# Two-stage packed attention with a gated feed-forward: leftover rows of four batches together, and half of batch 1's hidden columns, through seven products in place of whole products

## The chip, the cores and the metric

One Trainium2 chip, one of its cores. The metric is the device time of one execution in microseconds (us), the median of the runs shown; smaller is better. TensorE is PE here, and PEld its weight loads; VectorE is DVE, ScalarE is ACT, GpSimd is POOL, and SyncE is SP, whose queue issues nearly all DMAs. Each engine takes its own instructions in the order in which they stand.

## The reference, cut to what matters

```python
# 8 batches, 8 heads, 576 tokens, head_dim 64, 32 packed rows; d_model 512, d_ff 2048
def sm_attn(qq, kk, vv):
    s = scale * np.matmul(qq, kk.transpose(0, 1, 3, 2))
    a = np.exp(s - np.max(s, axis=-1, keepdims=True))
    a = a / (np.sum(a, axis=-1, keepdims=True) + 1e-09)
    return np.matmul(a, vv)
p_packed = sm_attn(p, k, v)
x = sm_attn(q, p_packed, p_packed)      # then (batch * tokens, 512)
h = x @ w_in                            # (4608, 2048)
out = (h * (1.0 / (1.0 + np.exp(-h)))) @ w_out
```

All of it is float32. The kernel writes a product of two float32 matrices as three products of a rounded upper part and the remainder (hi with hi, hi with lo, lo with hi).

## The kernel before

**Tiling.** Each batch's 576 tokens are two halves of 288. A half has 256 main rows (two blocks of 128) and 32 leftover rows. The 2048 hidden columns are 16 blocks f of 128 columns, or 8 pairs p of two blocks, or 4 quarters j of four blocks. PE makes a block of h for one half with six products of 288 columns (`h_products`, L615). ACT applies the gate. The leftover rows go to the tile `rest`, which has room for two batches (`b % 2`).

**Whole products.** For batches 0 and 1, each (batch, block) is a unit: `out_products` multiplies 128 x 128 blocks of the gated h by 512 columns of w_out, three terms for each of four row blocks, so 12 matmuls of 512 columns (L673). There are 32 such units. The sums of the first half of the columns are written to DRAM (`parts`) and added later.

**Seven products.** For batches 2 to 7, a unit is (batch, half, pair). The 2 x 2 blocks (two row blocks by two hidden blocks) times the 2 x 2 blocks of w_out (two hidden blocks by two column halves of 256) take seven block products, three terms each: 21 matmuls of 256 columns (`pair_products`, L673). What goes into them is combined first: on the side of h by three POOL instructions (`pair_sums`, L647 to L649), on the side of w_out once per pair on DVE, POOL and ACT (`pair_of_w`, `sums_of_pair`, `sums_upper`, `sums_lower`). The latter are kept in DRAM (`keep_sums`) and read back for each unit (`load_sums`, 768 KB) into a ring of four tiles; one of them replaces half of a block of w_out in SBUF (`first_in_place`). ACT rounds the seven combined blocks (`all_upper`, L663) and DVE makes the remainders (`all_lower`, L667). Four PSUM banks (`acc`) collect a half of a batch; then `pair_rows` (one ACT copy, L816, and five DVE additions, L815) makes the rows and stores them.

**Leftover rows.** After each odd batch, and once for batches 0 and 1, the 128 leftover rows of two batches go through `rest_products`: 16 blocks with three terms of 512 columns, 48 matmuls, in units of four blocks. `rest_rows` adds two banks where needed and stores four strips of 32 rows.

**Order.** `ORDER` is a string of some 1,700 steps that are recorded one by one, so that it sets the order on PE, DVE, ACT and SP by hand; POOL's order follows from it too. A step's letter names the function and its number the unit: B and G, N, I, F, L, O are `h_products`, the gate, leftover rows, `pair_sums`, `all_upper`, `all_lower` and `pair_products` (or the leftover products); E is `pair_rows`, Y `rest_rows`, S `load_sums`; r, R, ru, rl, rk and T are the steps of the sums of w_out.

Of the kernel before, what the change touches and what calls it, by code (L numbers as in the profile page):

```python
# [9 lines left out]
F32 = mybir.dt.float32  # L10
F32R = mybir.dt.float32r
# [8 lines left out]
P = 128  # L20
# [22 lines left out]
PACKS += [(b, j * FJ, FJ) for b in range(EARLY, B) for j in range(NJ)]  # L43
FROM_RING = [NJ] * EARLY + [2] + [0] * (B - EARLY - 1)
# [93 lines left out]
def packed_attention_ffn(ctx: ExitStack, tc: tile.TileContext, pkT, qT, v, w_in, w_out, out):  # L138
# [100 lines left out]
    class Weights:  # L239
# [8 lines left out]
        def fetch(self, n):  # L248
# [5 lines left out]
            elif place == "last":  # L254
                raw = self.tiles[n - 1][:, 2 * DM :]
            else:
                raw = win[:, place : place + 2 * nf].rearrange("p f i n -> p (f i n)")
# [689 lines left out]
```

## Time and profile before

| | |
|---|---|
| median of 3 runs | 680.04 us (679.95 to 680.74) |
| profiled execution | 681.22 us, of which the span is 679.4 us |
| busy | PE 97%, PEld 86%, DVE 63%, ACT 62%, POOL 34% of the span |
| DMA | 178.62 MB, mean 263 GB/s |

The page's busy share of PE is modelled and counts overlapping records, so the table alone doesn't say how close PE is to its limit; the distance between the starts of its matmuls does, and the chain of what released what shows where PE was itself the last to be waited for. The profiled execution is 1.18 us above the median. All sums are differences that are taken against its 679.4 us of span, and carried to the median.

### The profile page before, as it was taken

The numbers are of one execution on the slowest core, as the hardware profiler recorded it, in microseconds if no ns is written. First come the engines' busy times: TensorE is split into PE (matmuls) and PEld (weight loads), VectorE is DVE, ScalarE is ACT, GpSimd is POOL, SyncE is SP. The second block draws the span as 40 slices with busy tenths as digits, with TensorE's granted clock in tenths as the row PEclk, the third lists the DMA queues.
The fourth block names the chain that finished last, engine by engine and source line by source line (L and its number), as shares of the span: only waits on it lengthen the run. The fifth ranks groups of instructions, "written<-read, shape, count | busy, mean of one in ns | idle before, by whom it ended". The sixth has DMA issues, their size and how long they took to land.

```text
span 679.4 us, 14828 instructions
## 1 busy us (share of the span) xinstructions
PE 660.8 (97%) x5980; PEld 584.2 (86%) x5980; DVE 428.9 (63%) x595; ACT 423.3 (62%) x706; POOL 229.1 (34%) x337
## 2 busy tenths in 40 slices
PE   8898999999999999999999999999999999999997
PEld 6676778787878998899888998899988999899995
DVE  4999999987784356653576428763567426663433
ACT  4798876757557456764466638684367644766442
POOL 1111213243222543444242533445341343444440
PEclk9999999999999999999999999999999999999999
DMA  9748284968688669877798477977889278767441
GB/s 360 321 158 332 71 325 121 335 232 328 241 317 311 226 264 371 330 291 268 269 354 312 132 293 274 368 272 270 325 299 363 81 263 302 247 251 259 166 171 46
DMA packets 55107, 178.62 MB, mean 263 GB/s; under 512 B 21760, under 2 KB 25856, under 8 KB 47360
## 3 DMA queue, kind: packets, MB, share of 16 engines
q1 hardware_dynamic: 54944, 177.56, 70.9%
q8 instruction: 47, 0.77, 0.4%
q10 hardware_dynamic: 96, 0.13, 0.1%
q14 instruction: 20, 0.16, 0.1%
HBM read 149.42 MB, written 24.12 MB: 255 GB/s over the span
## 4 chain that ended last, share of the span: by engine, by line
PE 72%; DVE 9%; ACT 8%; DMA 4%; issue 4%; SPq 2%; POOL 1%; ACTq 0%; DVEq 0%; POOLq 0%
PE ps_acc L673 42%; PE ps_two L615 23%; PE ps_two L304 6%; DMA win<-in_w_out 2%; DVE g_lo L633 2%; SPq L388 2%; DMA sums_of_w<-sums_of_w 1%; ACT g_hi L663 1%; DVE g_lo L667 1%; DVE o L815 1%; PE ps_two L408 1%; ACT g L626 1%; DMA w_raw<-in_w_out 1%; ACT L188 1%; ACT g_hi L627 1%
## 5 line engine op out<-in xcount | busy, mean ns | idle before, releaser
L667 DVE TENSOR_TENSOR g_lo<-g,g_hi 128x896 fp32r<-128x896 f32 x96 | 108.5, 1134 | 132.5 <-ACT g_hi L663 129.7
L673 PE MATMUL ps_acc<-wo_hi,g_hi 128*128 128x256 f32 (+1 forms) x576 | 183.0, 318 | 0.7 <-DVE o L815 0.7
L673 PE MATMUL ps_acc<-wo_hi,g_lo 128*128 128x256 f32 (+1 forms) x576 | 182.1, 316 | 0.7 <-DVE g_lo L633 0.6
L673 PE MATMUL ps_acc<-wo_lo,g_hi 128*128 128x256 f32 (+1 forms) x576 | 181.4, 315 | 0.0
L615 PE MATMUL ps_two<-a_hi,pw_hi 128*128 128x288 f32 x512 | 152.0, 297 | 0.8 <-ACT tm L331 0.3
L615 PE MATMUL ps_two<-a_hi,pw_lo 128*128 128x288 f32 x512 | 150.9, 295 | 0.0
L615 PE MATMUL ps_two<-a_lo,pw_hi 128*128 128x288 f32 x512 | 150.6, 294 | 0.2 <-DVE a_lo L546 0.2
L647 POOL TENSOR_TENSOR g<-g 128x128 f32<-128x128 f32 x96 | 51.8, 540 | 273.1 <-ACT g L637 241.1
L663 ACT CAST g_hi<-g 128x896 fp32r<-128x896 f32 x96 | 90.0, 941 | 77.0 <-POOL g L649 40.6
L673 PEld LDWEIGHTS ps_acc<-wo_hi,g_hi 128*128 128x128 f32 x576 | 108.2, 188 | 14.8 <-issue 6.9
L673 PEld LDWEIGHTS ps_acc<-wo_hi,g_lo 128*128 128x128 f32 x576 | 108.3, 188 | 10.2 <-DVE g_lo L633 2.4
L673 PE MATMUL ps_acc<-sums_of_w,g_hi 128*128 128x256 f32 x576 | 115.6, 282 | 1.0 <-DMA sums_of_w<-sums_of_w 1.0
L673 PEld LDWEIGHTS ps_acc<-wo_lo,g_hi 128*128 128x128 f32 x576 | 108.2, 188 | 6.6 <-DVE wo_lo L297 0.3
L615 PEld LDWEIGHTS ps_two<-a_hi,pw_hi 128*128 128x128 f32 x512 | 96.3, 188 | 7.1 <-issue 3.0
L673 PEld LDWEIGHTS ps_acc<-sums_of_w,g_hi 128*128 128x128 f32 x576 | 87.8, 188 | 15.0 <-issue 13.3
L615 PEld LDWEIGHTS ps_two<-a_lo,pw_hi 128*128 128x128 f32 x512 | 96.4, 188 | 1.4 <-DVE a_lo L546 0.4
L615 PEld LDWEIGHTS ps_two<-a_hi,pw_lo 128*128 128x128 f32 x512 | 96.2, 188 | 0.0
L637 ACT ACTIVATE g<-ps_two 128x512 f32<-128x512 f32 x96 | 57.1, 598 | 42.9 <-PE ps_two L615 22.7
L673 PE MATMUL ps_acc<-sums_of_w,g_lo 128*128 128x256 f32 x288 | 80.0, 278 | 0.0
L648 POOL TENSOR_TENSOR g<-g 128x256 f32<-128x256 f32 x96 | 73.1, 763 | 6.5
L649 POOL TENSOR_TENSOR g<-g 128x128 f32<-128x128 f32 x96 | 56.7, 592 | 6.5
L673 PEld LDWEIGHTS ps_acc<-sums_of_w,g_lo 128*128 128x128 f32 x288 | 54.2, 188 | 0.4 <-DVE g_lo L667 0.4
(131 smaller groups left out, 838.1 us busy)
## 6 DMA issues: line engine op xcount, KB each, us to landing
sums_of_w<-sums_of_w SPq DMA_DIRECT2D x96, 768.0 KB, 6.4
w_quarter<-w_in SPq DMA_DIRECT2D x22, 1024.0 KB, 7.2
kvq_t<-in_v SPq DMA_DIRECT2D x8, 1280.0 KB, 9.3
kvq_t<-in_pkT SPq DMA_DIRECT2D x7, 1216.0 KB, 10.4
out<-o SPq DMA_DIRECT2D x16, 512.0 KB, 3.6
kvq_t<-in_qT SPq DMA_DIRECT2D x7, 1152.0 KB, 8.4
w_raw<-in_w_in SPq DMA_DIRECT2D x6, 1024.0 KB, 8.1
sums_of_w<-w_sums SPq DMA_DIRECT2D x8, 768.0 KB, 4.6
```

The lines of the kernel that those rows point to most:

```text
L188: nc.scalar.activation(ready, ident[:, :1], (AF.Exp, AF.Silu)[n])
L304: nc.tensor.matmul(bank(par)[NP * i : NP * i + NP], lhs(r, i), rhs(r, i), start=True, stop=True)
L388: nc.sync.dma_start(self.e1T[NP * at : NP * at + NP, : some.shape[1], i], some)
L615: nc.tensor.matmul(bank, p[:, par, cols], a[:, par], start=(n == 0), stop=(n == len(todo) - 1))
L633: nc.vector.tensor_tensor(g_lo[:, c], g[:, c], g_hi[:, c].bitcast(F32), ALU.subtract)
L637: nc.scalar.activation(g[:, : 4 * P].rearrange("p (e s) -> p e s", e=2), made["h", u, None][..., :MAIN], AF.Silu)
L647: nc.gpsimd.tensor_tensor(x[:, 4], x[:, 0], x[:, 2], ALU.subtract)
L648: nc.gpsimd.tensor_tensor(x[:, 5:7], x[:, 0:5:4], one, ALU.subtract)
L649: nc.gpsimd.tensor_tensor(x[:, 7], x[:, 3], x[:, 6], ALU.add)
L663: nc.scalar.copy(both[0], g)
L667: nc.vector.tensor_tensor(g_lo, g, g_hi.bitcast(F32), ALU.subtract)
L673: nc.tensor.matmul(out, g[:, rows], w, start=(first and n == 0), stop=(last and n == 2), skip_group_check=True)
```

## The change

Nothing in the arithmetic of the reference is left out. What changes:

- `WHOLE = 6`: 24 units of whole products stay (batch 0, and the first half of batch 1's columns). The second half of batch 1's columns becomes 8 units of seven products (2 halves x pairs 4 to 7), whose rows are added to what `parts` holds (`main_rows`).
- The leftover rows of four batches form 256 rows, so that they can go through seven products: 8 units for batches 0 to 3 and 8 for batches 4 to 7, in place of four groups of 48 matmuls. `keep_rest` writes the leftover rows of the first two batches of each four to DRAM, `load_rest` reads them back, `copy_rest` (two ACT copies per unit) puts both pairs of batches side by side. For the last eight of these units DVE does `pair_sums`, not POOL.
- The sums of w_out lie in four places of w_in's own buffer, which is free after the packs of batch 1; the last four pairs of a group that the next group begins with aren't read again (`PAIRS` turns the order), so 76 loads in place of 96.
- Batch 2 reads all of its w_in from DRAM (24 fetches in place of 22).
- `ORDER` is another string throughout. In the last unit the four banks end in another order (`final`), and the last store has eight strips, four of them issued by ACT.

```diff
+WHOLE = 6
+PAIRS = (0, 1, 2, 3, 4, 5, 6, 7), (4, 5, 6, 7, 0, 1, 2, 3)
+FROM_RING = [NJ] * EARLY + [0] * (B - EARLY)
...
-    units = [(b, f) for b, g in BLOCKS for f in range(g * FJ, g * FJ + FJ)]
+    units = [(b, f) for b, g in BLOCKS[:WHOLE] for f in range(g * FJ, g * FJ + FJ)]
     n_early = len(units)
-    units += [(0, f, "rest") for f in range(0, NF, FJ)]
+    units += [(1, (hf, p)) for hf in range(2) for p in range(NPAIR // 2, NPAIR)]
     for b in range(EARLY, B):
-        units += [(b, (hf, p)) for hf in range(2) for p in range(NPAIR)]
-        if b % 2:
-            units += [(b - 1, f, "rest") for f in range(0, NF, FJ)]
+        units += [(b, (hf, p)) for hf in range(2) for p in PAIRS[(b + hf + 1) % 2]]
+        if b % 4 == 3:
+            units += [(b - 3, ("rest", p)) for p in PAIRS[0]]
...
+    def copy_rest(u):
+        b, (_, p) = units[u]
+        g = hidden[u] = in_turn(gp_main, [P, 8 * P], F32, "g")
+        g = g[:, : 4 * P].rearrange("p (e r s) -> p r e s", e=2, r=2)
+        nc.scalar.copy(g[:, 0], made["rest", b // 4][:, 2 * p : 2 * p + 2])
+        nc.scalar.copy(g[:, 1], rest[:, 2 * p : 2 * p + 2].rearrange("p f e h s -> p f (e h s)"))
...
-        x = summed_tiles[b, hf, p] = in_turn(tp, [P, 2, 3 * HALF], F32R, "sums_of_w", TP_BUFS)
-        nc.sync.dma_start(x.bitcast(F32), sums_of_w[p])
+        if "sums" not in made:
+            made["sums"] = win_pool.tile([P, TP_BUFS * n], F32R, name="w_sum", tag=f"win_{NF - FJ}")
+        x = made["sums"][:, p % TP_BUFS * n : p % TP_BUFS * n + n]
+        summed_tiles[p] = x.rearrange("p (t n) -> p t n", t=2)
+        nc.sync.dma_start(summed_tiles[p].bitcast(F32), sums_of_w[p])
...
+    def rest_rows(n):
+        o = pair_rows(n, "rest", n == 1)
+        for k in range(2):
+            for m in range(4):
+                at = (4 * n + 2 * k) * S + m * HS + MAIN
+                (nc.scalar if n and m % 2 else nc.sync).dma_start(out[at : at + REST], o[m * REST : m * REST + REST, k])
```

Where this moves instructions is seen at three places. First PE at the program's end, where the last half of batch 7 gives way to leftover rows (`ps_acc_2221` to `2224` before and `1971` to `1974` after are the banks 0 to 3). Before:

```order
L673 MATMUL ps_acc_2224<-sums_of_w,g_hi 128x256 x2
L673 MATMUL ps_acc_2224<-sums_of_w,g_lo 128x256
L673 MATMUL ps_acc_2224<-wo_hi,g_hi 128x256
L673 MATMUL ps_acc_2224<-wo_lo,g_hi 128x256
L673 MATMUL ps_acc_2224<-wo_hi,g_lo 128x256
L673 MATMUL ps_acc_2221<-wo_hi,g_hi 128x512
L673 MATMUL ps_acc_2221<-wo_lo,g_hi 128x512
L673 MATMUL ps_acc_2221<-wo_hi,g_lo 128x512
L673 MATMUL ps_acc_2223<-wo_hi,g_hi 128x512
```

After, the last rows of PE's program:

```order
L689 MATMUL ps_acc_1971<-wo_hi,g_lo 128x256
L689 MATMUL ps_acc_1971<-w_sum,g_hi 128x256 x2
L689 MATMUL ps_acc_1971<-w_sum,g_lo 128x256
L689 MATMUL ps_acc_1974<-w_sum,g_hi 128x256 x2
L689 MATMUL ps_acc_1974<-w_sum,g_lo 128x256
L689 MATMUL ps_acc_1974<-wo_hi,g_hi 128x256
L689 MATMUL ps_acc_1974<-wo_lo,g_hi 128x256
L689 MATMUL ps_acc_1974<-wo_hi,g_lo 128x256
L689 MATMUL ps_acc_1973<-wo_hi,g_hi 128x256
L689 MATMUL ps_acc_1973<-wo_lo,g_hi 128x256
L689 MATMUL ps_acc_1973<-wo_hi,g_lo 128x256
```

Before, 48 matmuls of 512 columns into banks 0 and 2 stand at the end; after, eight times 21 matmuls of 256 columns into all four banks, the last three of them into bank 2.

Second, DVE at the same place. `g_lo` is the remainder that the next product needs, L815 the additions of `pair_rows`. Before, to the end of the program:

```order
L667 TENSOR_TENSOR g_lo<-rest,g_hi 128x512
L815 TENSOR_TENSOR o<-ps_acc_2222,o 128x2x256
L815 TENSOR_TENSOR o<-ps_acc_2221,o 128x256
L815 TENSOR_TENSOR o<-ps_acc_2224,o 128x256
L815 TENSOR_TENSOR o<-ps_acc_2223,o 128x256
L815 TENSOR_TENSOR o<-ps_acc_2224,o 128x512
L667 TENSOR_TENSOR g_lo<-rest,g_hi 128x512 x3
L800 TENSOR_TENSOR o<-o 128x256
L801 TENSOR_TENSOR o<-ps_acc_2223,o 128x512
```

After, from the additions that end batch 7 on (L653 to L655 are `pair_sums`):

```order
L815 TENSOR_TENSOR o<-ps_acc_1972,o 128x2x256
L815 TENSOR_TENSOR o<-ps_acc_1971,o 128x256
L815 TENSOR_TENSOR o<-ps_acc_1974,o 128x256
L815 TENSOR_TENSOR o<-ps_acc_1973,o 128x256
L815 TENSOR_TENSOR o<-ps_acc_1974,o 128x512
L653 TENSOR_TENSOR g<-g 128x128
L654 TENSOR_TENSOR g<-g 128x256
L655 TENSOR_TENSOR g<-g 128x128
L683 TENSOR_TENSOR g_lo<-g,g_hi 128x896 x2
```

Before, one remainder stands ahead of the five additions and three behind; after, the sums of a unit stand between the additions and the next remainder, and such sums go on to the end, which is five more additions in place of two.

Third, DVE where the last sums of w_out are made (`w_pair` and `w_sums` are the first and the last DVE step of a pair). Before:

```order
L768 TENSOR_TENSOR w_sums<-w_pair,w_sums 128x1024
L751 TENSOR_TENSOR w_pair<-wo_hi,wo_lo 128x2x256
L751 TENSOR_TENSOR w_pair<-wo_hi,wo_lo 128x512
L633 TENSOR_TENSOR g_lo<-g,g_hi 128x512
L530 TENSOR_TENSOR tm<-tm,sm 128x576
L534 STREAM_TRANSPOSE tm<-tm 128x576
L633 TENSOR_TENSOR g_lo<-g,g_hi 128x512
L768 TENSOR_TENSOR w_sums<-w_pair,w_sums 128x1024
L786 TENSOR_TENSOR o<-ps_acc,o 128x1024 x2
L667 TENSOR_TENSOR g_lo<-rest,g_hi 128x512
```

After, at the sixth pair's last step:

```order
L783 TENSOR_TENSOR w_sums<-w_pair,w_sums 128x1024
L766 TENSOR_TENSOR w_pair<-wo_hi,wo_lo 128x2x256
L766 TENSOR_TENSOR w_pair<-wo_hi,wo_lo 128x512
L587 TENSOR_TENSOR pw_lo<-ps_two,pw_hi 128x2x512
L683 TENSOR_TENSOR g_lo<-g,g_hi 128x896
L800 TENSOR_TENSOR o<-ps_acc,o 128x1024 x2
L527 TENSOR_REDUCE sm<-tm 128x18
L528 TENSOR_SCALAR sm<-sm 128x18
L529 RECIPROCAL sm<-sm 128x18
L783 TENSOR_TENSOR w_sums<-w_pair,w_sums 128x1024
L683 TENSOR_TENSOR g_lo<-g,g_hi 128x896
```

Before, all eight pairs' sums stand ahead of the first seven-product unit, and four units of leftover rows lie between; after, pairs 4 to 7 are made first, the last of them stands between the remainders of the first and the second such unit, and pairs 2 and 3 follow later.

## Rows read from the trace of the kernel before

**Rows 1.** The page's busy times (share, instructions) and its slices of granted clock.

```profile
PE 660.8 (97%) x5980; PEld 584.2 (86%) x5980; DVE 428.9 (63%) x595; ACT 423.3 (62%) x706; POOL 229.1 (34%) x337
...
PEclk9999999999999999999999999999999999999999
```

**Rows 2.** Chain in order of time: start us, us, what and how many.

```profile
134.32 2.95 PE ps_acc L673 x12
...
187.70 8.19 PE ps_acc L673 x36
...
217.78 2.39 PE ps_acc L673 x21
...
435.50 2.68 PE ps_acc L673 x21
...
441.34 4.78 PE ps_acc L673 x42
446.12 1.58 PE ps_two L615 x12
...
518.98 10.90 PE ps_acc L673 x48
```

**Rows 3.** PE by shape: busy us, mean ns | idle before us, what ended it.

```profile
L673 PE MATMUL ps_acc<-sums_of_w,g_hi 128*128 128x256 f32 x576 | 115.6, 282 | 1.0 <-DMA sums_of_w<-sums_of_w 1.0
...
L673 PE MATMUL ps_acc<-wo_hi,g_hi 128*128 128x512 f32 x192 | 76.8, 400 | 0.7 <-DVE o L815 0.7
```

**Rows 4.** Windows: us, then busy (count) of PE, PEld, DVE, ACT, POOL, PEclk, DMA share, GB/s.

```profile
0.00:20.00 20.00, 16.70 (x222) 13.88 (x223) 10.48 (x24) 10.15 (x19) 2.06 (x8) 1.00 0.92 367
...
20.00:140.00 120.00, 112.05 (x944) 88.06 (x943) 113.81 (x161) 94.65 (x162) 29.61 (x24) 1.00 0.65 236
0.00:217.78 217.78, 206.53 (x1689) 164.52 (x1690) 181.21 (x257) 156.32 (x263) 52.57 (x55) 1.00 0.72 268
```

**Rows 5.** DVE by shape, columns as in rows 3.

```profile
L667 DVE TENSOR_TENSOR g_lo<-g,g_hi 128x896 fp32r<-128x896 f32 x96 | 108.5, 1134 | 132.5 <-ACT g_hi L663 129.7 <-PE ps_two L615 2.5
...
L633 DVE TENSOR_TENSOR g_lo<-g,g_hi 128x512 fp32r<-128x512 f32 x28 | 25.5, 912 | 9.8 <-ACT g_hi L627 9.8
...
L815 DVE TENSOR_TENSOR o<-ps_acc,o 128x512 f32<-128x512 f32 x24 | 16.4, 684 | 7.1 <-ACT o L816 7.1
L815 DVE TENSOR_TENSOR o<-ps_acc,o 128x256 f32<-128x256 f32 x36 | 14.1, 421 | 1.7
...
L667 DVE TENSOR_TENSOR g_lo<-rest,g_hi 128x512 fp32r<-128x512 f32 x16 | 10.9, 683 | 10.3 <-ACT g_hi L663 10.3
...
L418 DVE TENSOR_TENSOR pp<-ps_two,rd 128x128 f32<-128x128 f32 x7 | 2.0, 285 | 5.5 <-PE ps_two L408 5.5
...
L800 DVE TENSOR_TENSOR o<-o 128x256 f32<-128x256 f32 x4 | 1.6, 412 | 3.5 <-ACT o L799 3.5
```

**Rows 6.** Chain of the last 20 us, columns as in rows 2.

```profile
662.46 0.38 ACT o L816
...
664.23 11.21 PE ps_acc L673 x48
...
675.46 0.70 DVE o L801
...
676.18 0.40 ACTq L808
...
676.63 0.43 ACTq L808
```

**Rows 7.** DMA issues: count, KB each, median us to landing.

```profile
sums_of_w<-sums_of_w SPq DMA_DIRECT2D x96, 768.0 KB, 6.4
...
sums_of_w<-w_sums SPq DMA_DIRECT2D x8, 768.0 KB, 4.6
...
out<-o ACTq DMA_DIRECT2D x2, 64.0 KB, 2.0
```

More of the change, by code (lines that the diff above doesn't have):

```diff
@@ L572, in upper @@
             if self.f % FJ == 0:
-                pool = pw_b if b >= EARLY and j >= 2 else pw
+                pool = pw_b if b >= EARLY and j < 2 else pw
                 both = [in_turn(pool, [P, 2 * JW + 2 * AT_PW], F32R, name) for name in ("pw_hi", "pw_lo")]
@@ L658, in all_upper @@
         g = all_of(u)
-        at = 0 if g.shape[1] > FJ * P else 64 - AT_G
         both = [in_turn(gp_main, [P, 7 * P], F32R, name) for name in ("g_hi", "g_lo")]
-        both = [t[:, at : at + g.shape[1]] for t in both]
         hidden[u] = g, *both
@@ L703, in packed_attention_ffn @@
     low, high = slice(0, HALF), slice(HALF, DM)
-    def rest_products(u):
-        b, f, _ = units[u]
-        first, last = f == 0, f + FJ == NF
-        for n in sorted(range(FJ), key=lambda n: n % 2) if last else range(FJ):
-            bank = 0 if n % 2 == 0 and (f + n) // 2 in summed else 2
-            begun = opened.get(("rest", b, bank))
-            opened["rest", b, bank] = True
-            products(acc[bank], u, f + n, n, not begun, last and n >= FJ - 2)
     opened = {}
@@ L718, in pair_products @@
         g_hi, g_lo = hidden[u][-2:]
-        last = p == NPAIR - 1
+        last = is_last(u)
+        final = last and u == len(units) - 1
         def term(bank, cols, at, w_hi, w_lo):
-            key = "pair", b, hf, bank
+            key = b, hf, bank
             begun = opened.get(key)
@@ L734, in pair_products @@
         term(0, high, 4, *t(2))
-        term(2, low, 6, *w(f2, high))
+        if not final:
+            term(2, low, 6, *w(f2, high))
         term(3, low, 1, *t(1))
         term(3, high, 3, *w(f1, high))
+        if final:
+            term(2, low, 6, *w(f2, high))
     summed_tiles = {}
@@ L794, in store, with pair_rows @@
         nc.sync.dma_start(out[at : at + MAIN].rearrange("(k p) e -> p k e", p=P), o)
-    def rest_rows(b):
-        o = in_turn(osb, [P, 2, DM], F32, "o")
-        if opened.get(("rest", b, 0)):
-            nc.scalar.copy(o[:, 1], acc[0])
-            nc.vector.tensor_tensor(o[:, 1, high], o[:, 1, high], o[:, 1, low], ALU.add)
-            nc.vector.tensor_tensor(o[:, 0], acc[2], o[:, 1], ALU.add)
-        else:
-            nc.scalar.copy(o[:, 0, low], acc[2][:, low])
-            nc.vector.tensor_copy(o[:, 0, high], acc[2][:, high])
-        for n in range(4):
-            at = b * S + n * HS + MAIN
-            rows = slice(n * REST, n * REST + REST)
-            (nc.scalar if n % 2 and b == B - 2 else nc.sync).dma_start(out[at : at + REST], o[rows, 0])
-    def pair_rows(b, hf):
+    def pair_rows(b, hf, final=False):
         o = in_turn(osb, [P, 2, DM], F32, "o")
```

226 lines of the change are left out of this document (123 added, 103 removed).

## The prediction

> **What bounds the kernel now.** I read the page's busy times first: PE is busy 97% of the span at full granted clock throughout (2.4 GHz), no other engine above 63% [rows 1]. A modelled busy share is not yet a bound, so I read the chain in order of time next, for the distance at which matmuls follow each other: 42 of 256 columns in 4.78 us, so 0.1138 us each; 48 of 512 columns in 10.90 us and 36 in 8.19 us, so 0.227 us each; 12 of 288 columns in 1.58 us [rows 2]. A whole product thus costs exactly two halves, and the time goes by columns. PE by shape shows how little PE stands still between these: a wait of 1.0 us in all ahead of the products with loaded sums, of 0.7 us ahead of the leftover products [rows 3]. So from about 40 us on the kernel is a string of matmuls with few gaps, and columns that are taken away come off the end, if the others keep up.
>
> Whether they can is asked where they are nearest to PE. That is DVE early on: it is busy 113.81 of the 120 us from 20 to 140, 95%, while it prepares the weights [rows 4]. Later it has much room (428.9 us in all).
>
> **The change part by part.** The sums are differences against the profiled execution's 681.22 us (span 679.4), which stands 1.18 us over the median; I carry them to the median of 680.04.
>
> *PE's columns.* Removed: 8 units of batch 1 with 12 matmuls each, and four groups of 48 for leftover rows, 288 of 512 columns: 288 x 0.227 = 65.4 us. Added: 8 + 16 units of 21, 504 of 256 columns: 504 x 0.1138 = 57.4 us. Net -8.0. The bounds are the prices of a run that begins after other work: 2.95 us for 12 instead of 2.73, 2.68 us for 21 instead of 2.39 [rows 2]. With all of batch 1's old units dear, 23.6 + 43.6 - 57.4: -9.8; with all new units dear, 65.4 - 64.3: -1.1. I take -8.0, since runs of both kinds stand between the same h products before and after.
>
> The Trainium skill has a rule against this: "TensorE: Matmul & The Clock Gate", section "Back-to-back issue gap", says that a stream of weight loads and matmuls settles at some 81 ns for 128 columns and 131 ns for 512. By it, 288 wide ones are 37.7 us and 504 halves, estimated from that page at 98 ns between those two, 49.4 us: +11.7. The trace disagrees with it (0.227 us for 512 columns), and the trace decides.
>
> *DVE early.* The first seven-product unit of batch 2 starts at 217.78 us now, and until then DVE is busy 181.2 us [rows 4]. Counted in the order, DVE has nearly the same ahead of that unit after: all weights, all eight pairs' sums and the same attention; 8 remainders of 896 columns more (9.1), 8 of 512 fewer (7.3), four of leftover rows fewer (2.7), two sets of five additions more (2 x (2 x 0.684 + 3 x 0.421) = 5.3), one set of leftover additions (1.1), a transpose and a pack remainder (2.0, an estimate from rows of like width) fewer: +1.3, so 182.5 us [rows 5]. But PE gets there sooner. Ahead of it stand 144 matmuls of 512 columns fewer (32.7), 170 of 256 more (19.3) and 12 of 288 fewer (1.6): 15.0 us, so at 202.8. By 140 us DVE has done 10.5 + 113.8 = 124.3 [rows 4]; the other 58.2 must fit into 62.8 us, 93%. The most that the trace shows over a long stretch is the 95% above; from 140 to 217.78 it was 56.9 of 77.8, 73%, when it had to wait for PE. I take 90%, since a unit's remainder waits for ACT's rounding and, here, POOL's sums: 64.7 us, +2.0. Bounds: -1 (a start that is a little earlier) to +8 (82%).
>
> In the same place stand the sums of pairs 4 to 7. The last is made just ahead of the second new product's remainder; from there it must be written (4.6 us) and read back (6.4 us) for the fourth product [rows 7], 11.0 us behind each other in SP's queue, with a read of `parts` between. PE has some 14.5 us of work from there if DVE is in time (three products at 2.39, four h products at 1.58, scores of an estimated 1.0), so it is hidden; if PE already waits for that remainder, the cover is 10.4 and a wait of 1 to 2 us shows. It is in the bounds above.
>
> *Leftover rows.* The two copies on ACT per unit (32, near 0.4 us each by the 0.38 us copy in rows 6) and the eight DMAs that keep and read rows are in stretches where ACT and DMA have room (ACT 62% busy); without that cover they would cost 12 us of ACT, in part. SP's queue gets these DMAs and two more weight fetches, and loses 20 of 96 loads of 768 KB [rows 7]. PE's 1.0 us of waiting for loads could go [rows 3]; against it two more groups now end in banks that the next product wants, and a dense run of leftover units makes each remainder follow the one before closely. I take +0.4, between -1 and +2.
>
> *DVE at the last group.* Behind the last half of batch 7 DVE has five additions (2.6 us), then one unit's sums (2 x 0.285 + 0.412 = 1.0, by the rows of like width) and a remainder (1.13), before the second leftover unit can go on [rows 5]. The copy and the first additions begin some 1.0 us before PE is through with that half, since banks 1 and 0 end nine matmuls early; so the remainder is there about 4.1 us after PE's last matmul of batch 7. PE has one unit (2.39), the wait for the first bank and two matmuls in the meantime, 2.7: a wait of 1.4. Before, the same place cost 0.7 by rows 3 and ended at 664.23 in rows 6. From there on a unit costs DVE 2.1 and PE 2.39, so it keeps up, with few tenths lost. +0.6, between 0 and +3.
>
> *The end.* Before, one addition of 0.70 us and ACT's two issues of 0.40 and 0.43 us stand behind PE's last matmul, then a landing of 2.0 [rows 6, 7]. After, five additions (2.6) and the copy (0.38) with 1.0 us of them ahead of PE's end: 2.0, so +1.3; four issues on ACT for two: +0.8. Together +2.1, between +1.3 and +2.6.
>
> Sum: -8.0 + 2.0 + 0.4 + 0.6 + 2.1 = -2.9, so 680.04 - 2.9 = **677.1** (the profiled execution 678.3).
>
> **The rivals.** *DVE keeps up.* For it: 95% over 120 us before, and 4.5 us of room in the count above. Against it: more engines stand in a row ahead of each remainder. Only columns and end count: -8.0 + 2.1 = -5.9, 674.1.
>
> *DVE is the bound until batch 2, but not by far.* At 85% the 58.2 us take 68.5 in place of 62.8, +5.7 in place of +2.0: 680.8, no change.
>
> *Slower: PE waits for DVE from 140 us to the first unit of batch 2.* For it: 73% there before. Against it: that was idle time for want of work. The point from which it decides is a busy share of 84%, where the wait (6.5 us) and the other terms eat up the columns; at 80% it is 72.8 us, +10.0: 685.1.
>
> *The products do not get cheaper.* If all 24 new units are dear (a run that is cut up by waits for remainders), columns give -1.1 only: 684.0. For it speaks that leftover units now need seven combined blocks each; against it that rows of 4.78 for 42 are the usual ones. The skill's rule named above would end on this side as well.
>
> **How the numbers follow.** Forecast, 675.4 to 678.6: 0.46. DVE keeps up, 672.6 to 675.4: 0.24. DVE the bound by a little, 678.7 to 681.3: 0.14. DVE the bound by far: 0.11. Products not cheaper: 0.05, of which 0.01 for the rule. No bound is under 672.6 but that of dear old units. The range of 8 in 10 is 672.6 to 681.5. What a measurement can tell from no change is about 0.2%, 1.4 us: faster 0.70, same 0.14, slower 0.16.
>
> **What would show it.** Right: products of 256 columns at 0.114 us, 504 more of them; DVE over 88% busy from 140 us to the first unit of batch 2, which starts near 205; a wait of PE of 1 to 2 us behind batch 7's last addition; some 6 us from PE's last matmul to the end where it is 4 now. Wrong: that unit starting behind 209 us (DVE), PE idle ahead of products with `w_sum` as the releaser (the loads), or new units at 2.6 us or more.

## The result: slower by 1.2%

| | before | after |
|---|---|---|
| median | 680.0 us (4 runs, 679.59 to 680.74) | 688.31 us (4 runs, 687.33 to 689.12) |
| ratio | | 1.012, 95% interval 1.0103 to 1.0138 |
| profiled execution, its span | 681.22 us, 679.4 us | 689.12 us, 687.3 us |

The forecast was 677.1 us, between 672.6 and 681.5. The page's busy times of the kernel after, beside [rows 1]:

```profile
PE 655.5 (95%) x6196; PEld 589.1 (86%) x6196; DVE 457.8 (67%) x631; ACT 426.0 (62%) x727; POOL 268.5 (39%) x385
```

PE is 5 us less busy and the span is 8 us longer, so PE waits. PE by shape says where, beside [rows 3] (columns as there); first the products for h in the kernel before, then the groups after:

```profile
L615 PE MATMUL ps_two<-a_hi,pw_hi 128*128 128x288 f32 x512 | 152.0, 297 | 0.8 <-ACT tm L331 0.3 <-ACT rest L628 0.3
```

```profile
L620 PE MATMUL ps_two<-a_hi,pw_hi 128*128 128x288 f32 x512 | 152.8, 299 | 7.8 <-ACT g L642 3.5 <-ACT rest L646 1.9 <-DVE tm L450 0.9
...
L689 PE MATMUL ps_acc<-w_sum,g_hi 128*128 128x256 f32 x720 | 144.5, 282 | 3.6 <-DMA w_sum<-sums_of_w 2.5 <-DVE o L815 1.2
...
L689 PE MATMUL ps_acc<-w_sum,g_lo 128*128 128x256 f32 x360 | 100.7, 280 | 2.9 <-DVE g_lo L683 2.9
```

The first products for h (L615 before, L620 after) waited for 0.8 us before; now it is 7.8 us, most of it for the gate on ACT (L642, L646). Where in time this is, the windows show (columns as in [rows 4]); first the kernel before, then after:

```profile
140.00:180.00 40.00, 40.00 (x270) 32.74 (x269) 31.59 (x41) 29.15 (x47) 11.39 (x11) 1.00 0.77 287
180.00:220.00 40.00, 40.00 (x278) 32.06 (x277) 26.67 (x36) 24.14 (x40) 10.51 (x15) 1.00 0.78 285
```

```profile
20.00:140.00 120.00, 113.00 (x949) 88.58 (x947) 115.64 (x162) 93.68 (x161) 31.88 (x24) 1.00 0.71 264
140.00:180.00 40.00, 34.26 (x246) 28.81 (x245) 30.06 (x36) 21.97 (x35) 20.86 (x24) 1.00 0.85 297
180.00:220.00 40.00, 36.55 (x333) 31.95 (x332) 34.37 (x41) 25.78 (x44) 22.54 (x30) 1.00 0.90 315
```

Up to 140 us the two kernels are alike. From 140 to 220 us PE (first pair of numbers) was never idle before, and is idle for 9.2 us of 80 after.

For the whole span I use PE's lag: the time at which a matmul starts, less the time that all matmuls ahead of it take at the spacings of [rows 2] (0.1138 us for 256 columns, and so on). It grows only where PE waits or where matmuls follow each other at more than these spacings. Its level depends on what the small products of the attention are priced at, so only its growth and the differences of the two kernels are read.

| | matmuls at full pace | lag at 160 us | at 220 | at 640 | at the last matmul | from there to the end |
|---|---|---|---|---|---|---|
| before | 640.4 | 23.6 | 24.2 | 33.4 | 34.8 | 4.4 |
| after | 632.3 | 21.9 | 34.9 | 45.4 | 48.7 | 6.45 |
| after less before | -8.1 | -1.7 | | | | +2.1 |
| growth from the column ahead | | | +12.4 | +1.3 | +1.9 | |

The terms add to +7.9 us, the difference of the spans. The columns came off as forecast, and 12.4 us were lost between 160 and 220 us: some 9 us are idle time of PE, the rest is matmuls at more than the usual spacing. Some 7 of the 12.4 us fall between 160 and 180 us.

### The profile page after: what moved, and what is told of

Same layout as the page of the kernel before. It is cut to its first block, busy times and chain, and to the rows that moved or that the text cites. A ratio compares the mean times of both kernels' runs of the same rounds, so it can differ in the third digit from the quotient of the medians.

```text
span 687.3 us, 15374 instructions
## 1 busy us (share of the span) xinstructions
PE 655.5 (95%) x6196; PEld 589.1 (86%) x6196; DVE 457.8 (67%) x631; ACT 426.0 (62%) x727; POOL 268.5 (39%) x385
## 4 chain that ended last, share of the span: by engine, by line
PE 64%; DVE 18%; DMA 6%; ACT 5%; issue 3%; POOL 3%; SPq 0%; DVEq 0%; ACTq 0%; POOLq 0%
PE ps_acc L689 37%; PE ps_two L620 22%; PE ps_two L310 4%; DMA w_sum<-sums_of_w 3%; DVE g_lo L683 2%; DVE o L815 2%; DMA first_sums<-w_sums 2%; ACT g_hi L679 1%; DVE g_lo L638 1%; DMA sums_of_w<-w_sums 1%; PE ps_two L414 1%; DVE win L291 1%; DVE w_raw L279 1%; DVE w_sums L783 1%; DVE w_raw L275 1%
## 5 line engine op out<-in xcount | busy, mean ns | idle before, releaser
L683 DVE TENSOR_TENSOR g_lo<-g,g_hi 128x896 fp32r<-128x896 f32 x120 | 137.5, 1150 | 142.2 <-ACT g_hi L679 140.0
L689 PE MATMUL ps_acc<-wo_hi,g_hi 128*128 128x256 f32 (+1 forms) x576 | 171.5, 298 | 1.2 <-DVE o L803 1.1
L689 PE MATMUL ps_acc<-wo_lo,g_hi 128*128 128x256 f32 (+1 forms) x576 | 170.4, 296 | 0.0
L679 ACT CAST g_hi<-g 128x896 fp32r<-128x896 f32 x120 | 112.3, 941 | 86.8 <-POOL g L655 54.1
L620 PE MATMUL ps_two<-a_hi,pw_hi 128*128 128x288 f32 x512 | 152.8, 299 | 7.8 <-ACT g L642 3.5
L653 POOL TENSOR_TENSOR g<-g 128x128 f32<-128x128 f32 x112 | 60.4, 539 | 247.5 <-ACT g L642 239.6
L620 PE MATMUL ps_two<-a_hi,pw_lo 128*128 128x288 f32 x512 | 151.2, 295 | 0.0
L620 PE MATMUL ps_two<-a_lo,pw_hi 128*128 128x288 f32 x512 | 150.7, 294 | 0.4 <-DVE a_lo L552 0.4
L689 PE MATMUL ps_acc<-w_sum,g_hi 128*128 128x256 f32 x720 | 144.5, 282 | 3.6 <-DMA w_sum<-sums_of_w 2.5
L689 PEld LDWEIGHTS ps_acc<-w_sum,g_hi 128*128 128x128 f32 x720 | 109.7, 188 | 20.1 <-issue 9.4
L620 PEld LDWEIGHTS ps_two<-a_hi,pw_hi 128*128 128x128 f32 x512 | 96.4, 188 | 17.8 <-PE ps_two L310 4.5
L689 PE MATMUL ps_acc<-w_sum,g_lo 128*128 128x256 f32 x360 | 100.7, 280 | 2.9 <-DVE g_lo L683 2.9
L620 PEld LDWEIGHTS ps_two<-a_lo,pw_hi 128*128 128x128 f32 x512 | 96.4, 188 | 1.3 <-DVE a_lo L552 0.6
L620 PEld LDWEIGHTS ps_two<-a_hi,pw_lo 128*128 128x128 f32 x512 | 96.3, 188 | 0.0
L642 ACT ACTIVATE g<-ps_two 128x512 f32<-128x512 f32 x104 | 61.4, 598 | 42.9 <-DVE g_lo L683 25.7
L654 POOL TENSOR_TENSOR g<-g 128x256 f32<-128x256 f32 x112 | 85.1, 762 | 7.4
L655 POOL TENSOR_TENSOR g<-g 128x128 f32<-128x128 f32 x112 | 72.4, 649 | 7.5
L689 PEld LDWEIGHTS ps_acc<-w_sum,g_lo 128*128 128x128 f32 x360 | 67.7, 188 | 4.2 <-DVE g_lo L683 3.9
```

The costliest lines, as they stand in the source:

```text
L620: nc.tensor.matmul(bank, p[:, par, cols], a[:, par], start=(n == 0), stop=(n == len(todo) - 1))
L642: nc.scalar.activation(g[:, : 4 * P].rearrange("p (e s) -> p e s", e=2), made["h", u, None][..., :MAIN], AF.Silu)
L653: engine.tensor_tensor(x[:, 4], x[:, 0], x[:, 2], ALU.subtract)
L654: engine.tensor_tensor(x[:, 5:7], x[:, 0:5:4], one, ALU.subtract)
L655: engine.tensor_tensor(x[:, 7], x[:, 3], x[:, 6], ALU.add)
L679: nc.scalar.copy(both[0], g)
```

## What PE waits for between 140 and 220 us

Pairs are numbered from 0, and the changed kernel makes their sums in the order 0, 1, 4, 5, 6, 7, 2, 3; those of 0, 1 and 4 are done by 140 us, and the five others are called late here. (The section on the change says that 4 to 7 are made first: 0 and 1 stand ahead of them.) What the expectations call the sixth and the seventh pair are pairs 6 and 7.

What PE waited for from 140 to 220 us (waited for, us in total, times, longest us), after; before, that list is empty:

```profile
PE ps_two L620 <- ACT g L642: 3.5, 1, 3.5
PE ps_two L620 <- ACT rest L646: 1.9, 2, 1.2
PE ps_acc L689 <- DVE g_lo L683: 1.5, 2, 1.3
PE ps_acc L689 <- DMA w_sum<-sums_of_w: 1.0, 1, 1.0
```

Two more waits for DVE, of 0.8 and 0.4 us, make it 9.1 us: 5.4 for ACT, 2.7 for DVE, 1.0 for a load.

The chain in order of time, after, from the write of pair 5's sums past the first product that reads pair 7's sums back (at 186.12 us; columns as in [rows 2]; L779 is ACT's rounding of a pair's sums, L783 DVE's remainder, L771 to L774 POOL's sums of w_out, L653 to L655 the sums of h, L679 the rounding of the combined blocks):

```profile
145.16 11.18 DMA first_sums<-w_sums
...
156.45 1.06 ACT w_sums L779
...
157.53 1.24 DVE w_sums L783
...
160.23 0.74 POOL w_pair L771
...
162.67 0.73 POOL w_pair L774
163.40 0.43 POOL g L653
...
165.20 0.95 ACT g_hi L679
...
167.18 2.35 DVE o L800 x2
...
170.74 1.66 DVE w_sums L783
...
172.42 7.42 DMA sums_of_w<-w_sums
...
179.85 6.23 DMA w_sum<-sums_of_w
...
195.38 1.39 DVE w_sums L783
196.78 1.54 DVE g_lo L683
198.31 1.47 DVE w_pair L766 x2
```

There is one tile `w_sums`. ACT can't round the next pair's sums until the two writes of the pair before have landed. The one of 256 KB takes 11.2 us here; in the kernel before its median was 4.7:

```profile
first_sums<-w_sums SPq DMA_DIRECT2D x8, 256.0 KB, 4.7
```

Behind that rounding in ACT's order stands the gate of the first seven-product unit, then comes POOL, which sums pair 7 of w_out ahead of that unit's blocks, and ACT waits again, with the gate of the next unit behind it. PE's h products run out of PSUM tiles. (In the written order that unit's sums, I24, stand ahead of pair 7's, R7. `ORDER` fixes PE, DVE, ACT and SP alone, so POOL took them the other way round; the section on the kernel before says that POOL's order follows from it, which does not hold here.) The waits of ACT from 140 to 220 us, after:

```profile
ACT g_hi L679 <- POOL g L655: 7.3, 3, 4.2
ACT w_sums L779 <- DMA first_sums<-w_sums: 4.5, 1, 4.5
...
ACT w_sums L779 <- POOL w_pair L774: 3.0, 1, 3.0
```

ACT's two longest groups in the same stretch before were for PE and for DVE:

```profile
ACT g L626 <- PE ps_two L615: 7.0, 4, 3.9
ACT g L626 <- DVE g_lo L633: 4.1, 3, 2.3
```

That speaks for a row of waits (theory A) and against DVE as the bound (theory B, the forecast's). It is not the whole case: DVE is 75% and 86% busy in the two windows, and the chain lies mostly on DVE from 193 to 202 us. The runs tell the two apart.

## The experiments

Each is the changed kernel with the edit that its text names; e4 and e5 take back half of the change, and e12, e16 and e18 join edits. "Over before" is the difference from the runs of the kernel before on the same chip.

| | median us | over before | ratio, 95% interval |
|---|---|---|---|
| changed kernel | 688.31 | +8.3 | 1.012 (1.0103 to 1.0138) |
| e1 POOL in written order | 687.09 | +7.3 | 1.0105 (1.008 to 1.013) |
| e2 sums in place | 687.34 | +7.6 | 1.011 (1.0095 to 1.0125) |
| e3 later loads | 687.14 | +7.4 | 1.0109 (1.0094 to 1.0124) |
| e4, e5 batch 1 whole | 697.71, 700.23 | +17.9, +19.9 | 1.0277 (1.0252 to 1.0302), 1.0298 (1.0281 to 1.0316) |
| e6 less DVE, 3 pairs | 688.46 | +8.1 | 1.0121 (1.0073 to 1.0168) |
| e7 e6 and e3 | 685.73 | +5.4 | 1.0078 (1.0061 to 1.0095) |
| e8 parts on POOL | 687.63 | +7.3 | 1.0102 (1.0086 to 1.0118) |
| e9 no late sums | 681.04 | +0.4 | 1.0008 (0.9998 to 1.0018) |
| e10 last sums on POOL | 691.36 | +10.7 | 1.0158 (1.0142 to 1.0173) |
| e11 more PE | 691.9 | +11.3 | 1.0154 (1.0129 to 1.0179) |
| e12 mends | 693.46 | +12.8 | 1.0192 (1.0177 to 1.0207) |
| e13 less DVE, 5 pairs | 687.34 | +6.5 | 1.0095 (1.0076 to 1.0114) |
| e14 no POOL sums | 687.12 | +6.3 | 1.0099 (1.0083 to 1.0115) |
| e15 no writes | 686.91 | +6.1 | 1.0094 (1.0078 to 1.0109) |
| e16 mends 2 | 685.72 | +4.9 | 1.0077 (1.0061 to 1.0094) |
| e17 e14 and e15 | 681.84 | +1.7 | 1.0029 (1.0018 to 1.004) |
| e18 ACT's order | 686.89 | +6.8 | 1.0092 (1.0079 to 1.0105) |

Most times lie inside a range that was stated for them or up to 0.5 us outside the nearer one. e7 and e13 fit none of theirs, e10 lost more than its text allowed, and e4, e5 and e12 lie far above what was hoped for.

### One wait at a time, with the whole result: e1, e2, e3, e8

> POOL takes its instructions in the order of the written steps; only this differs from the changed kernel (688.3 us). There the sums of the first seven-product unit stood on POOL behind the sums of w_out of the seventh pair, which came late. Theory A (the row of steps that makes the sums of w_out for pairs 5 to 7 is what PE waits for between 160 and 220 us: one tile that is free only when its write has landed, POOL's order, the read back): PE's first wait of 4.0 us falls to about 1, but the seventh pair's sums come some 2 us later and with them the wait for the loaded sums; 685 to 687 us. Theory B (DVE has too much work until batch 2, and every wait removed ahead of it comes back as one for DVE): within 1 us of 688.3.

```diff
-engines={E.PE, E.DVE, E.Activation, E.SP}
+engines={E.PE, E.DVE, E.Activation, E.SP, E.Pool}
```

> The sums of pairs 6 and 7 are made where they are needed: three quarters in their place of w_in's buffer, the fourth in w_out's block. They are still written to DRAM for later, but nobody waits for that write, and they are not read back for the first use. Theory A: ACT's wait of 4.5 us for the write of the pair before goes, and so does the wait of PE for the loaded sums of pair 7 (1.2 us); 682 to 685 us. Theory B: DVE has one instruction more for each of the two pairs and nothing less, so 687.5 to 689 us.

In `sums_upper`, for pairs 6 and 7:

```diff
+x = made["x", p] = made["sums"][:, p % TP_BUFS * n : p % TP_BUFS * n + n].rearrange("p (t n) -> p t n", t=2)
+nc.scalar.copy(x[:, 0], r[:, : 3 * HALF])
+nc.scalar.copy(wo_hi[:, 2 * p, high], r[:, 3 * HALF :])
...
```

> Two DMAs of 1.0 and 1.2 MB (the last quarter of w_in on its way out, and the k of batch 3) are issued behind the writes of the sums of pairs 5 and 6, where they stood ahead of them or at their side. Theory A: the write of pair 5 lands in 6 to 7 us in place of 11.2, ACT's wait for it (4.5 us) falls under 1, and the first wait of PE by up to 3; 685 to 687 us. Theory B: 688 us as before, since the work of DVE is the same.

```diff
-aM2.1 x3 B24 rk5 ru6 o22 l23 o23 Z0. aN2.1 k3 G24
+aM2.1 B24 rk5 x3 ru6 o22 l23 o23 Z0. aN2.1 G24
-pf11 rk6 I25
+pf11 rk6 k3 I25
```

> Batch 1's two additions of the stored first half of its columns (1.45 and 1.23 us on DVE at 191.8 and 209.9 us, each ahead of a remainder that PE waits for) go to POOL; only the store waits for them. Theory B: PE's waits behind them fall by 1.5 to 2.5 us, 685.8 to 687. Theory A: under 0.7 us, since POOL is behind ACT there and makes the next sums later.

```diff
-nc.vector.tensor_tensor(o, o, outs.pop(("o", b, hf)), ALU.add)
+nc.gpsimd.tensor_tensor(o, o, outs.pop(("o", b, hf)), ALU.add)
```

Each came out some 1 us under the changed kernel, with intervals that overlap its own, so none is a gain that is clear by itself. The profiles say why. In e2 and e3 PE's wait for the gate at 164 us fell from 3.5 to 2.2 and 2.1 us and the one of 1.0 us for pair 7's loaded sums went, but 0.9 us of waiting for the banks that `main_rows` frees came in its place. In e1 POOL made the first unit's blocks early, and ACT's 7.3 us of waiting for them went; but ACT then stood 8.3 us in two waits for landed writes (4.5 in the changed kernel) and 2.8 for POOL's sums of w_out (3.0), and PE's longest wait, now 4.0 us, came a few us later. In e8 PE's waits for DVE's remainders fell from 1.5 to 0.3 us, and the 3.5 us for the gate stayed. This fits neither theory well: waits move along the row.

### Half of the change alone: e4, e5

> One half of the change alone: batch 1's columns stay whole products as in the kernel before, the leftover rows of four batches go through seven products as in the changed one; the steps stand as in the kernel before until batch 2, and as in the changed one behind it (which half of the pairs comes first is exchanged). Columns: 192 of 512 less (43.6 us), 336 of 256 more (38.2), -5.4 us against the kernel before. Theory A or B: the loss between 160 and 220 us is from batch 1's half, so it is gone here; with +2.1 at the end and some 3 us of waits further on 679.5 to 682 us. Rival C (the leftover rows and what they need, the loads among it, make the loss): 685 us or more.

> As e4 (batch 1's columns as whole products, leftover rows of four batches through seven), with two things put right: the four DMAs that keep the leftover rows of batches 4 and 5 follow the exchange of the pairs' halves (in e4 some rows were stored too early), and the first packs of batch 2 are fetched and made some 20 us earlier, since in e4 PE waited 3.7 us for fetches of w_in, and the lag that e4 took between 190 and 240 us (16 us, with 0.72 of the clock at its lowest) was from there. If batch 1's half is what costs the 12 us between 160 and 220 us: 680 to 684 us, with PE's lag at 220 us within 3 of the kernel before. If leftover rows cost it: above 686.

```diff
-WHOLE = 6
+WHOLE = 8
-PAIRS = (0, 1, 2, 3, 4, 5, 6, 7), (4, 5, 6, 7, 0, 1, 2, 3)
+PAIRS = (4, 5, 6, 7, 0, 1, 2, 3), (0, 1, 2, 3, 4, 5, 6, 7)
-    units += [(1, (hf, p)) for hf in range(2) for p in range(NPAIR // 2, NPAIR)]
...
```

By their times both lie on the rival's side, far above it even. To 180 us the lag is that of the kernel before (23.3 and 23.0), so the loss at 160 to 180 us is from batch 1's half. Then both lose 16 to 19 us by 240 us. The longest of PE's waits there are for w_in, which the packs of batch 2 need, 3.7 us in e4 and 7.2 in e5; the rest is shorter waits for ACT and DVE, and the granted clock fell (0.76 and 0.83 from 200 to 220 us). PE's waits in e5 from 180 to 240 us:

```profile
PE ps_two L309 <- DMA w_quarter<-w_in: 7.2, 2, 3.9
```

The changed kernel reads all of batch 2's w_in from DRAM into one buffer, and the leftover rows of batches 0 and 1, which stood there before and probably gave time for it (no run takes that apart), have moved to batch 3. What the leftover rows' part would bring under an order of its own stays open.

### The sums of w_out: e9, e6, e13, e14, e15, e17, e7

> The sums of w_out of pairs 5, 6, 7, 2 and 3 are left out altogether (on DVE, POOL and ACT, with their writes and the reads into w_out's blocks); where they would be read, those of pair 4 are, so the number and size of the reads stay. Batches 1 to 7 are wrong by that. Theory D (it is the making of these sums, on whichever engine, beside the first seven-product units that takes the 12 us between 160 and 220; DVE's part and the writes' part are each only a piece, as e6, e3 and e7 show): PE's lag at 220 us falls from 34.9 to 24 to 27, 678 to 681 us. Rival E (the eight units would lose it even so: the row ACT, POOL, ACT, DVE for each unit is too long for PE's pace): lag above 30, 683 or more.

The two lines in the middle stand at the head of the six functions that make a pair's sums, `pair_of_w` to `first_in_place`.

```diff
+LEFT_OUT = (5, 6, 7, 2, 3)
...
+        if p in LEFT_OUT:
+            return
...
-        nc.sync.dma_start(summed_tiles[p].bitcast(F32), sums_of_w[p])
+        nc.sync.dma_start(summed_tiles[p].bitcast(F32), sums_of_w[4 if p in LEFT_OUT else p])
```

7.9 of 8.3 us are gone, and the lag at 220 us is 27.5. So the making of these five pairs' sums beside the first seven-product units is what makes the kernel slower than before. It is not the whole of the 12.4 us: e9 still loses some 3.5 us more than the kernel before between 160 and 220 us, nearly all of it behind 180 us. With the later terms that uses up the 8.1 us of columns, so even without these sums the change gains nothing. Then each of its parts alone:

> DVE's additions and remainders for the sums of w_out of pairs 7, 2 and 3 are cut to 16 of 256 columns each (the sums are wrong there, and batches 1 to 7 with them); every other engine and every DMA is left as it is in the changed kernel. DVE has 6 us less between 160 and 206 us (per pair 0.69 + 0.69 + 1.23 down to some 0.6). Theory B (DVE is the bound there): PE's lag at 220 us falls by 4 to 6 us, 682 to 684 us. Theory A (the chain of waits for DMA, POOL and ACT): less than 1.5 us, 686.5 to 688.

> e6 for all five late pairs (5, 6, 7, 2, 3): DVE's three instructions for each are cut to 16 of 256 columns, POOL, ACT and every DMA stay, in the same order; the sums are wrong by it. 2.0 us of DVE less for each pair, 10 us in all. All five left out on every engine gave 7.3 us (e9). If DVE alone made that loss: 681 to 682.5 us, PE's lag at 220 us near 27.5. If it is one of several: 684 to 686.5, lag 30 to 33.

```diff
+            n = SHORT if p in (5, 6, 7, 2, 3) else HALF
-            nc.vector.tensor_tensor(to, each(wo_hi, f), each(wo_lo, f), ALU.add)
+            nc.vector.tensor_tensor(to[..., :n], each(wo_hi, f)[..., :n], each(wo_lo, f)[..., :n], ALU.add)
...
```

> POOL's four instructions for the sums of each of the five late pairs are left out (3.0 to 3.7 us each, 16 us in all); DVE, ACT and all DMAs stay, and the sums are wrong. If POOL's share in the row is what holds the first units' combined blocks and with them ACT and PE: 682 to 685 us, and the first wait of 3.7 us at 164 us gone. If POOL only passes on what DVE and the writes make late: 686.5 or more.

> The writes of the sums of the five late pairs and the reads into w_out's blocks are left out, with SP's waits for them; the loads read the sums of pair 4 in their place (wrong sums). DVE, POOL and ACT do all they did. If waiting for landed writes is the larger part: 682 to 685 us, lag at 220 us under 31. If it is as small as in e2 and e3, where only its longest waits were taken: 686 to 687, lag 32 to 33.

Both leave out a function's body for the five pairs, as in e9: `sums_of_pair` in e14, `keep_sums` and `first_in_place` in e15, where the loads read pair 4's sums instead. (In e6, e7, e13 to e15 and e17 `w_pair` and `w_sums` are also allocated once, not anew for each pair.) Each of e13, e14 and e15 is within 2.2 us of the changed kernel, with intervals that overlap its own; e6 gave nothing that can be told from it. The waits of ACT from 140 to 220 us say what is next late, in e14:

```profile
ACT w_sums L785 <- DMA first_sums<-w_sums: 7.7, 3, 3.7
```

and in e15:

```profile
ACT g_hi L680 <- POOL g L656: 7.1, 3, 4.0
```

Without POOL's sums ACT stands longer for the writes (4.5 us in the changed kernel); without the writes it stands for POOL as long as there (7.3), and 4.5 us in place of 3.0 for POOL's sums of w_out. So both had to go:

> e14 and e15 together: for the five late pairs POOL's sums and the writes (with the reads into w_out's blocks) are left out; DVE and ACT do all their work for them, 10 us of DVE and 5 of ACT. Alone they gave 1.1 and 1.4 us, the same cut on DVE 1.0, all together (e9) 7.3. If what PE waits for is ACT, which stands in its order for POOL's sums and for landed writes with the gate of the next block behind it: 680.5 to 682.5 us, lag at 220 us under 29, although DVE has its full work. If DVE's work is a limit of its own behind these two: 684 us or more, lag above 31.

It gave 6.6 of the 8.3 us, with all of DVE's work in place. DVE in the stretch from 140 us to the first unit of batch 2 (columns as in [rows 4]), changed kernel, then e13, then e17:

```profile
140.00:210.35 70.35, 63.15 (x519) 53.51 (x517) 57.59 (x70) 41.74 (x69) 39.23 (x48) 1.00 0.86 298
```

```profile
140.00:209.53 69.53, 64.21 (x521) 55.32 (x519) 47.21 (x70) 42.53 (x72) 35.94 (x48) 0.98 0.88 314
```

```profile
140.00:202.28 62.28, 62.18 (x521) 53.59 (x519) 55.69 (x70) 42.10 (x71) 27.41 (x32) 1.00 0.70 256
```

Each ends where that unit starts: 210.4, 209.5 and 202.3 us. In e13 DVE has 10 us less to do and is busy 68%, and PE is hardly sooner (at a clock of 0.98). In e17 DVE has its full work, is busy 55.69 of 62.28 us, 89%, and PE is idle for 0.1 us. Theory B falls as the main cause. The loss at 160 to 180 us goes with POOL's sums and the writes, and the step between them and PE is ACT, which stood for both; e17 takes the two out together with the read-back of the late sums, so it doesn't price them one by one. The longest wait of PE that is left in e17 is for DVE, just behind that stretch, and as long as in the changed kernel:

```profile
PE ps_acc L690 <- DVE g_lo L684: 1.3, 1, 1.3
```

> e6 and e3 together: less DVE work, and the two large DMAs behind the writes of sums. e3 alone gave 1.2 us. If both limits take turns (a wait for a landed write first, then DVE), the gains add or more than add: 680.5 to 683 us. If DVE alone is the bound, e3's part is lost in it: as e6, within 0.7. If the chain alone is: as e3, 687.

With 6 us less of DVE and the later loads the time is 5.4 us over before, a gain of 2.9 us where e6 and e3 alone had 0.2 and 0.9, so DVE's part does shorten the row where the writes are not ahead of it. It is a link in the row, and not its limit.

### What a reserve PE has there: e11

> In the eight seven-product units of batch 1 the first block's six products for h are done twice (48 matmuls of 288 columns more, 6.3 us of PE between 153 and 215 us; the result stays). If PE is not the bound there, as all theories but one say, most of it falls into waits: 0 to 3 us more than the changed kernel. If PE's own pace sets the end there too: 6 us more, 694.

```diff
+            if n_early <= u < n_early + 8 and at == 0:
+                for n, (p, a, par) in enumerate(todo):
+                    nc.tensor.matmul(ps[:, at, :HS], p[:, par, cols], a[:, par], start=(n == 0), stop=(n == len(todo) - 1))
```

3.0 us more over before than the changed kernel, for 6.3 us of added PE work. So about half of it fell into waits (the two intervals overlap, so the share is rough). The other half may lie in the row itself, since each unit's gate now comes some 0.8 us later; no run shows that.

### The last leftover units: e10

> For the last eight leftover units the combined blocks are made on POOL, as for all other units, not on DVE. In the changed kernel PE waits 1.3 us there for banks that DVE's five additions free and then 0.9 us for a remainder that stands behind these additions and a unit's sums. If that row on DVE is the wait, POOL can make the second unit's sums beside the additions: 0.5 to 1.0 us less in the last 30 us. If POOL is too slow (2.0 us for a unit where PE takes 2.39, and a copy, a rounding and a remainder behind it), PE waits some tenths for each of the eight units: up to 2 us more.

```diff
-engine = nc.vector if units[u][0] == B - 4 and units[u][1][0] == "rest" else nc.gpsimd
+engine = nc.gpsimd
```

2.4 us more over before: PE's waits in the last stretch grow from 2.1 to 3.4 us, and come back at later units. DVE is the better engine for these sums.

### Putting it right with the whole result: e12, e16, e18

> All that e1, e2, e3, e8 and e10 changed, together, with the whole result: sums of pairs 6 and 7 made in place, the two large DMAs later, batch 1's added parts and the last sums on POOL, POOL in written order. If the limits take turns, gains of 1.2 to 2.5 us for each piece alone that was half hidden add up to 4 to 5: 683 to 685 us. If one limit is left that none of these touches: 686 or more.

> The whole result, with three of the edits of e12: sums of pairs 6 and 7 made in place, the two large DMAs later, batch 1's added parts on POOL; without POOL in written order (in e12 the parts stood ahead of batch 2's first sums on POOL, and PE waited 4.6 us) and with the last sums on DVE (POOL cost 3.0 us in e10). If the pieces add: 684 to 685.5 us, still slower than before. If the parts on POOL get in the way again: 687 or more.

> e16 with another order on ACT at the first two seven-product units, the whole result: the first unit's gate stands ahead of the rounding of the sixth pair's sums, and the second unit's gates ahead of the rounding of the first unit's combined blocks, so ACT doesn't stand for POOL or a write with the gate behind it; POOL takes the first unit's sums ahead of the seventh pair's. If that row on ACT is what PE waits for at 160 to 175 us: PE's wait of 2.2 us there goes, and 682.5 to 684.5 us. If it only moves to the next place in the row: 685 to 686.5.

```diff
-Z0. aN2.1 G24 rl6 r7 pu10 pl10 T5 N24 aX2.1 D1 I24 R7 B25 F24 N25 G25 pf11
+Z0. aN2.1 G24 N24 ru6 rl6 r7 pu10 pl10 T5 aX2.1 D1 I24 R7 B25 G25 N25 F24 pf11
```

e12 took the edits of e1, e2, e3, e8 and e10 together and was the worst of these: apart from e10's loss, POOL stood idle for 6.5 us for DVE's last row of batch 1, then added the parts (2.34 us), and only then made batch 2's first sums, which stood behind that in the written order. PE's waits from 200 to 225 us:

```profile
PE ps_acc L690 <- ACT g_hi L680: 4.6, 1, 4.6
```

e16 left out the edits of e1 and e10 and gained 3.4 us, the most with the whole result. In e18 PE's wait of 2.2 us for the gate went, others came (2.0 us in all for ACT's leftover rows, L647), and it was not faster than e16. So the order on ACT alone is not the cause: as long as POOL's sums and the writes are there, the wait moves to the next place in the row. No version with the whole result beats the kernel before.

## Why the prediction was wrong, step by step

**PE's columns: right.** -8.0 forecast, -8.1 by the counts. The chain after, beside [rows 2], has one unit at 2.39 and two at 4.78 us as before:

```profile
217.22 2.39 PE ps_acc L689 x21
...
313.77 4.78 PE ps_acc L689 x42
```

So "the products do not get cheaper" is out. With it goes, for this kernel, the rule in the Trainium skill's "TensorE: Matmul & The Clock Gate", section "Back-to-back issue gap".

**DVE early: the step that failed.** The forecast took the place right: the first unit of batch 2 at 202.8 us if nobody holds PE (202.3 in e17). DVE's work up to there was right too, 58.2 us forecast and 57.59 measured. It then priced every wait there as a busy share of DVE: 93% needed, 90% taken, +2.0. The measured term is +12.4. The rival with 80% came near in the number, 685.1 us, since DVE was busy 82% up to 210.35 us, but its cause is refuted by e13 and e17: 89% was to be had. So that nearness is luck. The sign of being wrong "that unit starting behind 209 us (DVE)" came true in its time, 210.35 us, and not in its cause. The sentence "since a unit's remainder waits for ACT's rounding and, here, POOL's sums" named the row and didn't price it. The order showed that ACT's rounding of a pair's sums stands ahead of gates, that it needs the tile of the pair before back from a write, and that POOL's share of `w_pair` now meets units that need POOL as well. Before, no such unit stood there, and from 140 us on none of ACT's longer waits was for a landed write or for these sums. Of the 12.4 us, e9 and e17 tie some 9 to this row; the 3.5 us left over are not taken apart, but for the 1.3 us of a DVE remainder.

The working has a slip here: a share of 84% is said to be where the wait and the other terms eat up the columns. By its own terms a wait of 4.9 us does that, at 86%; 84% gives +1.6 us.

**The sums of pairs 4 to 7: right place, too small.** Written and read back in 11.0 us by [rows 7]; the chain shows 7.42 + 6.23 = 13.65 and a wait of 1.0 us, the lower end of the 1 to 2 us that were allowed if PE already waited. The median of such a write is 7.3 us after, not 4.6, as the DMA issues show:

```profile
w_sum<-sums_of_w SPq DMA_DIRECT2D x76, 768.0 KB, 6.2
...
sums_of_w<-w_sums SPq DMA_DIRECT2D x8, 768.0 KB, 7.3
...
first_sums<-w_sums SPq DMA_DIRECT2D x8, 256.0 KB, 7.3
```

Durations of DMAs were taken from a kernel in which other transfers stood beside them.

**Leftover rows, +0.4:** +1.3 from 220 to 640 us, within its bounds. **DVE at the last group, +0.6:** +1.9, within its bounds. The place is the one named; PE's waits from 655 us on, after:

```profile
PE ps_acc L689 <- DVE o L815: 1.2, 1, 1.2
PE ps_acc L689 <- DVE g_lo L683: 0.9, 1, 0.9
```

The banks are waited for as well as the remainder.

**The end, +2.1: right in sum.** 6.45 us from the last matmul's start to the end, 4.38 before. The two parts miss in opposite ways: the first store is issued 0.86 us later behind the last matmul's start than before (+1.3 forecast), and from there to the end it takes 1.21 us longer (+0.8). The chain after, beside [rows 6]:

```profile
680.16 0.38 ACT o L816
...
680.56 0.70 DVE o L815
...
681.36 0.77 DVE o L815 x2
...
682.15 0.69 DVE o L815
```

**Size of it all.** With +12.4 in the place of +2.0 and the smaller terms as measured, the forecast's own sum is -8.1 + 12.4 + 1.3 + 1.9 + 2.1 = +9.6; the kernel was 1.7 us ahead by 160 us in the profiled execution, which leaves +7.9. The range ended at 681.5 because I gave the case "DVE the bound by far" 0.11, and had no case for ACT.

## What to carry to other kernels

A busy share says whether an engine has the time, not whether it is in time: where units of a new kind start, follow one unit through every engine's queue and ask at each step what stands ahead of it and what that waits for. A tile that is free only when a DMA has landed puts that DMA's time, under the load of that moment, into the queue of the engine that writes the tile next, and onto all that is queued behind (ACT stood for 4.5 us here). Where several waits run beside each other, taking out one shows little; take out two or all of them before a suspect is cleared.

## What the runs showed of the hardware

The granted clock fell after long waits of PE in some executions and not in others. In e14 PE was busy for 2.20 of the 5 us from 165 us on, and the clock of the next 5 us was 0.50, the lower level (windows, columns as in [rows 4]):

```profile
165.00:170.00 5.00, 2.20 (x17) 1.97 (x15) 2.43 (x5) 1.58 (x4) 1.50 (x3) 0.92 0.87 339
170.00:175.00 5.00, 4.88 (x33) 3.96 (x34) 4.79 (x8) 3.75 (x6) 4.73 (x5) 0.50 1.02 314
```

The changed kernel's profiled execution kept 1.00 there after a longer idle time of PE, 3.5 us against 2.9 in e14. Of the profiled executions, those of e1, e6, e8, e10 to e14 and e16 show the lower level between 167 and 180 us, and those of the kernel before, the changed kernel, e2, e3, e7, e9, e15, e17 and e18 do not show it there. What it costs is not shown. e6's four runs lie between 684.82 us at a mean clock of 0.996 and 692.75 at 0.988; but the changed kernel's slowest run, 689.12 us, has the highest mean clock of its four, 0.999, and e14 took 686.52 us at 0.996 and 686.67 at 0.990. So how much of a gain the clock hid in e13 and e14 stays open.

The two writes of a pair's sums (768 and 256 KB) took 4.6 and 4.7 us to land by their medians before, and 7.3 both after. From 140 us on they took 3.6 to 4.9 us before and 4.3 to 11.2 after; the longest before was 10.5 us, at 133 us. The DMA share from 140 to 180 and from 180 to 220 us is 0.85 and 0.90 after, 0.77 and 0.78 before.
